# Where the x of the final addition comes from: four selecting matmuls from the norm's rows, in place of a second load

## The chip, the cores and the metric

The kernel runs on one core of a Trainium2 chip. A core has five engines with instruction queues of their own: TensorE (PE: matmuls, and PEld, its loads of weights), VectorE (DVE), ScalarE (ACT), GpSimd (POOL) and SyncE (SP). Sixteen DMA engines move data between the chip's memory and the core's SBUF. The metric is the device time of one execution in microseconds; lower is better.

## The reference

One decoding step for two sequences with a model width of 448: layer norm, attention over the last 2048 positions of a cache with 8 K/V heads of 256 and 16 query heads, and a gate from a two-layer network with relu. The attention's output is multiplied by the gate, and x is added.

```python
x = A_x                                   # (2, 1, 448)
xn = _layernorm(x, axis=-1)
# attention: q = xn @ wq, 16 heads of 256, W = 2048 of 8192 cached positions,
# softmax(q k^T / 16) v, then @ wo (4096 x 448)
s = _A_ref(xn, A_k_cache, A_v_cache, A_wq, A_wo)
# gate: silu(relu(xn @ w1) @ w2), w1 448 x 1792, w2 1792 x 448
g = _silu(_B_ref(xn, B_w1, B_w2))
return x + s * g
```

## The kernel before

The kernel writes one list of instructions for each engine (`_Prog`); an engine works its list in order and waits on semaphores for what an instruction depends on. Every instruction is recorded through the same helpers, so the profile names all DMA issues L36 and all matmuls L249.

**Loads.** SP issues, in this order: wq into `vbuf1` (L194), w1 and w2 into `vbuf0` (L195, L196), the K tiles 0 and 1 into `kbuf0` and `kbuf1`, then V 0, K 2, V 1, K 3, V 2, V 3 (`load_k`, `load_v`, L187 to L192), each as soon as the last reader of its buffer is done, and last wo in four parts into `kbuf0` (from L510). K and V come as four tiles of 4 MB each: a tile holds 32 stretches of 64 positions for each of four pairs of sequence and head on the 128 partitions.

**x.** ACT's queue begins with two loads of x. The first (L176) puts the two rows of 448 into partitions 0 and 1 of `x_sb`, for the norm. The second (L178, `d_xc`) puts x into `x_c` in the layout of the output: eight pieces of 112 numbers, piece i of row b in partition 32 i + 16 b. POOL clears `x_c` first (L177).

**Norm.** DVE takes mean and variance from `x_sb` (L212, L213), ACT the square root (L216), DVE the scaled rows `xg` (L219). PE turns them into columns in the PSUM bank `mbk` (L253), and DVE writes them to `xr` (L255). Between L219 and L255, DVE's list has the small constants made from the identity: `par8`, `wrow`, `wcol` (L230), `qmask` (L233), `fold`, `gsum`.

**Zeroing.** Before the square root ACT clears three PSUM banks (L210), `obk0`, `obk1` and `fbk`, since the matmuls with a column position write 4, 16 or 17 partitions of each group of 32.

**Body.** `do_q` multiplies wq (it waits for wq, `xr` and the cleared `obk0`). `do_H` (two halves), its transposes and `do_F` make the gate's input in `fbk`: four groups of 112 columns at partitions 0, 32, 64 and 96, 17 rows each, of which row 0 belongs to sequence 0 and row 16 to sequence 1. `do_gate` (ACT's exp at L328, then DVE) leaves the gate in `g_sb`. Then, for each K tile, DVE transposes it in eight steps (`do_T`, L343) and PE makes the scores (`do_S`); the softmax (`chain`) and the products with V (`do_PV`) of one tile run beside the scores of the next.

**End.** After the last V tile, 128 matmuls multiply wo into `fbk` (32 row groups, four column positions), DVE multiplies by the gate (L532) and adds `x_c` (L534), and ACT issues the store (L536).

`st` holds the last operation on each shared buffer, so that the next writer waits for it. It starts as `st = {"mbk": v_xr}` (L259): `fbk` has no earlier user than the zeroing, and `do_H` waits for that through `a_z[2]`.

Of the kernel before, what the change touches and what calls it, by code (L numbers as in the profile page):

```python
# [5 lines left out]
BF = mybir.dt.bfloat16  # L6
F32 = mybir.dt.float32
ACT = mybir.ActivationFunctionType
ALU = mybir.AluOpType
AX = mybir.AxisListType  # L10

PE, DVE, ACTE, SP, POOL = "pe", "dve", "act", "sp", "pool"
# [62 lines left out]
def bass_recurrent_scan__sliding_block_cached__dense_activation_relu__decode_kernel(  # L75
# [11 lines left out]
    B, Sq, D = A_x.shape  # L87
# [16 lines left out]
    NCOL = D // 4  # L104
# [4 lines left out]
    with es:  # L109
        pr = _Prog(nc, es)  # L110

        def named(name, shape, dt):
            return es.enter_context(nc.sbuf_tensor(name, shape, dt))

        def psum(name, shape, dt):
            return es.enter_context(nc.psum_tensor(name, shape, dt))

        def view(t, off, dims, n=128, p0=0, pstep=1):
            width = t.shape[1]
            return bass.AP(t, p0 * width + off, [[width * pstep, n]] + dims)  # L120

        ident = named("ident", [128, 128], BF)
# [10 lines left out]
        x_sb = named("x_sb", [128, D], BF)  # L133
# [7 lines left out]
        qbd = [named(f"qbd{i}", [128, QW], BF) for i in range(2)]  # L141
        h_n = named("h_n", [128, FC], BF)
        h_sb = named("h_sb", [128, 32], BF)
        x_c = named("x_c", [128, NCOL], BF)
        ea = named("ea", [128, NCOL], F32)
        g_sb = named("g_sb", [128, NCOL], F32)
        tmp = named("tmp", [128, NCOL], F32)
        out_sb = named("out_sb", [128, NCOL], BF)
# [20 lines left out]
        fbk = psum("fbk", [128, 512], F32)  # L169
        mbk = psum("mbk", [128, 512], F32)  # L170
        nbk = psum("nbk", [128, 512], F32)

        def kv_src(k, cache):
            return cache.rearrange("b h s d -> (b h) s d")[k::NQ, SK - W:SK, :].rearrange("g (i t) d -> i g (t d)", t=NT)

        d_x = pr.dma(ACTE, x_sb[0:B, :], A_x[:, 0, :])  # L176
        p_xc = pr.op(POOL, lambda e: e.memset(x_c[:, :], 0.0))  # L177
        d_xc = pr.dma(ACTE, view(x_c, 0, [[1, NCOL]], n=8, pstep=16),  # L178
                      A_x[:, 0, :].rearrange("b (i n) -> i b n", i=4), [p_xc])
        d_k, d_v = {}, {}  # L180

        wq_src = A_wq.rearrange("r (hf c) -> (r hf) c", hf=2).rearrange("(p s) c -> p (s c)", s=SLOTS)
# [7 lines left out]
        def load_v(k):  # L190
# [8 lines left out]
        p_id = pr.op(POOL, lambda e: e.affine_select(  # L199
            out=ident[:, :], in_=ident[:, :], compare_op=ALU.not_equal, fill=1.0,  # L200
            base=0, pattern=[[-1, 128]], channel_multiplier=1), [i0])
        i1 = pr.op(POOL, lambda e: e.memset(ident_f[:, :], 0.0), [p_id])
        p_idf = pr.op(POOL, lambda e: e.affine_select(
            out=ident_f[:, :], in_=ident_f[:, :], compare_op=ALU.not_equal, fill=1.0,
            base=0, pattern=[[-1, 128]], channel_multiplier=1), [i1])
        p_one = pr.op(POOL, lambda e: e.memset(one_f[:, :], 1.0), [p_idf])
        p_hz = pr.op(POOL, lambda e: e.memset(h_sb[:, :], 0.0))
        p_qz = [pr.op(POOL, lambda e, t=t: e.memset(t[:, :], 0.0)) for t in qbd][-1]

        a_z = [pr.op(ACTE, lambda e, t=t: e.memzero(t[:, :])) for t in (obk[0], obk[1], fbk)]  # L210
# [4 lines left out]
            out=sd[0:B, 0:1], in0=st2[0:B, 1:2], scalar1=EPS, scalar2=None, op0=ALU.add), [v_ag])  # L215
        a_sd = pr.op(ACTE, lambda e: e.activation(sd[0:B, 1:2], sd[0:B, 0:1], ACT.Sqrt), [v_ve])  # L216
        v_rs = pr.op(DVE, lambda e: e.reciprocal(rstd[0:B, :], sd[0:B, 1:2]), [a_sd])
        for e2 in range(2):
            v_xn = pr.op(DVE, lambda e, e2=e2: e.tensor_scalar(  # L219
                out=view(xg, 128 - 127 * e2, [[256, 4], [128, 2], [2, 64]], n=B),  # L220
                in0=view(x_sb, 3 * e2, [[1, 4], [0, 2], [SLOTS, 64]], n=B),
# [3 lines left out]
            out=par2[:, :], in_=view(ident, 0, [[1, 2], [2, 64]]), axis=AX.X, op=ALU.add), [p_id])  # L225
# [4 lines left out]
        v_wc = pr.op(DVE, lambda e: e.tensor_scalar(  # L230
            out=view(wcol, 0, [[4, 128], [1, 4]], n=4), in0=view(ident, 0, [[0, 128], [1, 4]], n=4),
            scalar1=1.0, scalar2=BIG, op0=ALU.subtract, op1=ALU.mult))
        v_qm = pr.op(DVE, lambda e: e.tensor_reduce(  # L233
            out=qmask[:, :], in_=view(ident, 0, [[32, 4], [1, 32]]), axis=AX.X, op=ALU.add))

# [12 lines left out]
        def mm(out_ap, lhsT, rhs, start, stop=False, **kw):  # L248
            return lambda e: e.matmul(out_ap, lhsT=lhsT, rhs=rhs, start=start, stop=stop,  # L249
                                      skip_group_check=True, **kw)  # L250

        for s in range(SLOTS):
            m_xr = pr.op(PE, mm(mbk[:, 2 * s:2 * s + 2], xg[0:B, 128 * s + 128:128 * s + 256], ident[0:B, 0:B], s == 0),  # L253
                         [v_xn, p_id])
        v_xr = pr.op(DVE, lambda e: e.tensor_tensor(  # L255
            out=view(xr, 0, [[4, SLOTS], [2, 2], [1, 2]]), in0=view(mbk, 0, [[2, SLOTS], [0, 2], [1, 2]]),
            in1=view(par8, 0, [[1, SLOTS], [1, 2], [0, 2]]), op=ALU.mult), [m_xr, v_par8])

        st = {"mbk": v_xr}  # L259

        def do_q():
            deps = [d_wq, v_xr, a_z[0]]
# [253 lines left out]
        deps = [st["at", NQ - 1], v_fold]  # L516
        for b in range(2):
            m_at = pr.op(PE, mm(mbk[:, 256 + 32 * b:288 + 32 * b], at_exp[:, 128 * b:128 * b + 128],
                                fold[:, :], b == 0, b == 1), deps + [st["mbk"]])
            deps = []  # L520
        v_at2 = pr.op(DVE, lambda e: e.tensor_copy(at2[:, :], mbk[:, 256:320]), [m_at])  # L521
        deps = [v_at2, st["g"]]
        landed = dict(d_wo)
        for j in range(32):
            deps = deps + [landed.get(j)]
            for i in range(4):
# [4 lines left out]
                deps = []  # L531
        v_t = pr.op(DVE, lambda e: e.tensor_tensor(  # L532
            out=tmp[:, :], in0=fbk[:, 0:NCOL], in1=g_sb[:, :], op=ALU.mult), [m_o, st["g"]])
        v_o = pr.op(DVE, lambda e: e.tensor_tensor(  # L534
            out=out_sb[:, :], in0=tmp[:, :], in1=x_c[:, :], op=ALU.add), [v_t, d_xc])
        d_o = pr.dma(ACTE, out[:, 0, :].rearrange("b (i n) -> i b n", i=4),  # L536
                     view(out_sb, 0, [[1, NCOL]], n=8, pstep=16), [v_o])
        pr.op(SP, None, [d_o])
# [30 lines left out]
```

## Time and profile before

| | us |
|---|---|
| median of 3 runs | 110.84 |
| the three runs | 110.48, 110.84, 110.93 |
| the profiled execution | 110.73 |
| its span, first to last instruction | 109.3 |

| engine | busy, us | share of the span |
|---|---|---|
| PE matmuls | 63.9 | 58% |
| PE loads of weights | 26.0 | 24% |
| DVE | 57.6 | 53% |
| ACT | 12.4 | 11% |
| POOL | 9.0 | 8% |

The page gives busy times of the engines, 40 equal slices of the span with the busy share of each in tenths, the DMA queues (q1 is SP's, q10 ACT's, q8 and q14 carry instructions), the chain of work that ended last, and groups of instructions. A timeline row has the start, the duration, the engine, the line, the operation with its output and input, and in brackets how long the engine was idle before it and what ended that. A row of windows has the busy time and count for PE, PEld, DVE, ACT and POOL, the granted clock of TensorE, the busy share of the DMA engines and their GB/s.

### The profile page before, as it was taken

To read this page: it belongs to the slowest core of one execution; us is meant where nothing else is said; L and a number is where in the kernel's file an instruction comes from. 1 tells how busy PE (TensorE), PEld (TensorE's weight loads), DVE (VectorE), ACT (ScalarE), POOL (GpSimd) and SP (SyncE) were. 2 spreads that over 40 slices of the span, in tenths; PEclk is the share of its full clock that TensorE was granted. 3 is DMA by queue.
4 is the path that set the end of the run, shared out by engine and by line. 5 is a ranking of instruction groups with operands and counts; after the bars stand their busy time and mean duration, and the time that the engine had idled before them with its cause. 6 is when DMAs were issued, how large, how long until landed. Compare 5 with 4: busy or idle time off the path is not lost.

```text
span 109.3 us, 1328 instructions
## 1 busy us (share of the span) xinstructions
PE 63.9 (58%) x554; PEld 26.0 (24%) x554; DVE 57.6 (53%) x95; ACT 12.4 (11%) x24; POOL 9.0 (8%) x45
## 2 busy tenths in 40 slices
PE   0010655764089897849481999683089949009491
PEld 0000113133033222323130334241034214003190
DVE  2165047320399999987435999242399943100202
ACT  2970000000000000200050000032000004100200
POOL 6500000720000004000500000000000000000000
PEclk9999999999556999999996559999959999955559
DMA  6898999999999999999999999999999999999940
GB/s 169 346 483 355 431 404 510 408 432 504 390 396 444 492 396 396 456 480 396 399 480 438 396 408 492 432 396 408 504 420 396 420 498 408 396 405 414 407 171 1
DMA packets 2321, 44.19 MB, mean 404 GB/s; under 512 B 266, under 2 KB 396, under 8 KB 908
## 3 DMA queue, kind: packets, MB, share of 16 engines
q1 hardware_dynamic: 2288, 44.11, 94.6%
q8 instruction: 4, 0.07, 0.2%
q10 hardware_dynamic: 28, 0.01, 0.0%
q14 instruction: 1, 0.01, 0.0%
HBM read 44.11 MB, written 0.00 MB: 403 GB/s over the span
## 4 chain that ended last, share of the span: by engine, by line
DMA 70%; DVE 12%; PE 12%; SPq 3%; issue 1%
DMA kbuf<-in_A_k_cache_dram 42%; DMA kbuf<-in_A_wo_dram 28%; DVE kt L343 10%; PE sbk L249 9%; SPq L36 3%; PE obk L249 2%; DVE tmp L331 1%; DVE rm L361 1%; PE mbk L249 0%; PE nbk L249 0%; PE fbk L249 0%; DVE mx L371 0%; DVE tmp L532 0%; PE mbk L366 0%; DVE out_sb L534 0%
## 5 line engine op out<-in xcount | busy, mean ns | idle before, releaser
L249 PE MATMUL sbk<-kt,qbd 128*128 128x512 bf16 x128 | 36.2, 432 | 15.0 <-DVE kt L343 14.5
L343 DVE STREAM_TRANSPOSE kt<-kbuf 128x1024 f32<-128x1024 f32 x32 | 36.9, 1210 | 8.9 <-DMA kbuf<-in_A_k_cache_dram 8.7
L249 PEld LDWEIGHTS sbk<-kt,qbd 128*128 128x128 bf16 x128 | 12.3, 107 | 37.2 <-DVE kt L343 22.5
L249 PE MATMUL obk<-vbuf,pt 128*16 128x512 bf16 x128 | 9.3, 442 | 4.6 <-DMA vbuf<-in_A_v_cache_dram 4.6
L292 POOL COPY qbd<-qall 32x32 bf16<-32x32 bf16 x32 | 5.7, 204 | 44.1 <-PE sbk L249 28.3
L383 ACT ACTIVATE bias<-mbk 128x1 f32<-128x1 f32 x4 | 0.7, 171 | 58.6 <-PE mbk L249 58.6
L433 DVE TENSOR_TENSOR at_exp<-nbk,qmask 128x16 bf16<-128x16 f32 x16 | 1.7, 166 | 10.5 <-PE nbk L249 10.5
L249 PE MATMUL obk<-vbuf,xr 128*4 128x512 bf16 x28 | 3.2, 626 | 3.8 <-DMA vbuf<-in_A_wq_dram 3.8
L392 DVE STREAM_TRANSPOSE pt<-e_sb 128x512 bf16<-128x512 bf16 x4 | 2.8, 711 | 4.7 <-ACT e_sb L387 4.7
L271 DVE TENSOR_SCALAR kt<-obk 128x1024 bf16<-128x1024 f32 x2 | 2.4, 1218 | 5.6 <-PE obk L249 5.6
L249 PEld LDWEIGHTS obk<-vbuf,pt 128*16 128x16 bf16 x128 | 3.1, 98 | 8.5 <-DMA vbuf<-in_A_v_cache_dram 4.7
L249 PE MATMUL mbk<-ident,xg 2*128 2x2 bf16 x7 | 0.3, 164 | 7.9 <-DVE xg L219 7.9
L361 DVE TENSOR_REDUCE rm<-sbk 128x1 f32<-128x512 f32 x4 | 2.7, 682 | 4.0 <-PE sbk L249 4.0
L249 PE MATMUL fbk<-vbuf,xr 128*4 128x448 bf16 x14 | 4.3, 461 | 0.7 <-DVE h_n L304 0.7
L416 ACT ACTIVATE o_sb<-obk,rs 128x512 bf16<-128x512 f32 x4 | 2.7, 687 | 11.1 <-PE obk L249 11.1
L249 PE MATMUL fbk<-kbuf,at 128*17 128x112 bf16 x128 | 3.1, 282 | 0.4 <-DVE at L521 0.3
L249 PEld LDWEIGHTS fbk<-kbuf,at 128*17 128x17 bf16 x128 | 2.7, 128 | 0.7 <-DVE at L521 0.4
L304 DVE TENSOR_SCALAR h_n<-fbk 4x448 bf16<-4x448 f32 x2 | 1.2, 612 | 3.0 <-PE fbk L249 3.0
L387 ACT ACTIVATE e_sb<-sbk,bias 128x512 bf16<-128x512 f32 x4 | 2.7, 687 | 0.1
L249 PE MATMUL mbk<-one_f,mrow 1*128 1x1 f32 x8 | 1.5, 256 | 1.9 <-DVE mrow L374 1.9
L366 PE MATMUL mbk<-ident_f,rm 128*1 128x128 f32 x4 | 1.1, 270 | 2.4 <-DVE rm L361 2.4
L249 PE MATMUL nbk<-fold,o_sb 128*128 128x8 bf16 x16 | 1.0, 170 | 2.2 <-ACT o_sb L416 2.2
(63 smaller groups left out, 34.4 us busy)
## 6 DMA issues: line engine op xcount, KB each, us to landing
kbuf<-in_A_k_cache_dram SPq DMA_DIRECT2D x4, 4096.0 KB, 27.0
vbuf<-in_A_v_cache_dram SPq DMA_DIRECT2D x4, 4096.0 KB, 26.4
vbuf<-in_A_wq_dram SPq DMA_DIRECT2D x1, 3584.0 KB, 11.2
vbuf<-in_B_w_dram SPq DMA_DIRECT2D x2, 1568.0 KB, 16.2
kbuf<-in_A_wo_dram SPq DMA_DIRECT2D x1, 1904.0 KB, 28.2
kbuf<-in_A_wo_dram SPq DMA_DIRECT2D x1, 1008.0 KB, 30.0
kbuf<-in_A_wo_dram SPq DMA_DIRECT2D x1, 448.0 KB, 30.6
kbuf<-in_A_wo_dram SPq DMA_DIRECT2D x1, 224.0 KB, 30.7
```

The lines of the kernel that those rows point to most:

```text
L36: o = _Op(eng, lambda e: e.dma_start(dst, src), [d for d in deps if d is not None], True)
L249: return lambda e: e.matmul(out_ap, lhsT=lhsT, rhs=rhs, start=start, stop=stop, skip_group_check=True, **kw)
L271: v = pr.op(DVE, lambda e, par=par: e.tensor_scalar(out=view(kt, 128 * par, [[256, 8], [32, 4], [1, 32]]), in0=view(obk[0], par, [[64, 8], ...
L292: st["qbd", k] = pr.op(POOL, lambda e, a=a, b=b: e.tensor_copy(view(qbd[k % 2], 24 + 32 * a + 4 * b, [[2, 2], [128, 8], [1, 2]], n=32, p0= ...
L304: st["h_n"] = pr.op(DVE, lambda e: e.tensor_scalar(out=h_n[0:4, u * (FC // 2):(u + 1) * (FC // 2)], in0=fbk[0:4, 0:FC // 2], scalar1=0.0, ...
L343: st["T", k, e] = pr.op(DVE, lambda e: e.transpose(view(dst, lo, [[128, NT // 2], [1, 32]]), view(src, lo, [[128, NT // 2], [1, 32]])), deps)
L361: st["rm", k] = pr.op(DVE, lambda e: e.tensor_reduce(out=rm[k % 2][:, :], in_=sbk[k % 2][:, :], axis=AX.X, op=ALU.max), [st["S", k, 7], st ...
L366: st["rmT", k] = pr.op(PE, lambda e: e.matmul(mbk[0:1, 0:128], lhsT=rm[k % 2][:, :], rhs=ident_f[:, :], start=True, stop=True, is_transpos ...
L387: st["exp", k] = pr.op(ACTE, lambda e: e.activation(e_sb[k % 2][:, :], sbk[k % 2][:, :], ACT.Exp, bias=bias[k % 2][:, 0:1], accum_out=ssum ...
L392: st["pt", k] = pr.op(DVE, lambda e: e.transpose(pt[k % 2][:, :], e_sb[k % 2][:, :]), [st["exp", k], st.get(("PV", k - 2))])
L416: st["osb", k] = pr.op(ACTE, lambda e: e.activation(o_sb[k % 2][:, :], obk[k % 2][:, :], ACT.Copy, scale=rs[:, k:k + 1]), [st["PV", k], st ...
L433: st["at", k] = st["nbk"] = pr.op(DVE, lambda e, b=b, h=h: e.tensor_tensor(out=view(at_exp, 128 * b + 64 * h + 16 * k, [[4, 2], [8, 2], [1 ...
```

## The change

The second load of x and the memset of its tile go. In their place a small matrix `sel` of ones and zeros is made: POOL clears its two rows, and DVE copies the 2 x 2 identity into its columns 0 and 16. Four matmuls, one for each 112 columns, multiply `sel` (2 x 17) with the raw rows of `x_sb` and write 17 rows at partitions 0, 32, 64 and 96 of `fbk`: row 0 is sequence 0, row 16 sequence 1, as in the gate. ACT copies the bank's 112 columns on all partitions to `x_c`, which is now a tile of f32. `fbk`'s next user waits for that copy, and the final addition for it instead of the load. The matmuls stand between the norm's transposes and `do_q` in PE's list; the copy to `sel` stands between `wcol` and `qmask` in DVE's; ACT's copy stands between the square root and the gate's exp.

```diff
@@ -141,7 +141,8 @@
         h_sb = named("h_sb", [128, 32], BF)
-        x_c = named("x_c", [128, NCOL], BF)
+        sel = named("sel", [128, 32], BF)
+        x_c = named("x_c", [128, NCOL], F32)
@@ -174,9 +175,6 @@
         d_x = pr.dma(ACTE, x_sb[0:B, :], A_x[:, 0, :])
-        p_xc = pr.op(POOL, lambda e: e.memset(x_c[:, :], 0.0))
-        d_xc = pr.dma(ACTE, view(x_c, 0, [[1, NCOL]], n=8, pstep=16),
-                      A_x[:, 0, :].rearrange("b (i n) -> i b n", i=4), [p_xc])
@@ -204,6 +202,7 @@
+        p_sz = pr.op(POOL, lambda e: e.memset(sel[0:B, :], 0.0))
         p_hz = pr.op(POOL, lambda e: e.memset(h_sb[:, :], 0.0))
@@ -230,6 +229,7 @@
+        v_sel = pr.op(DVE, lambda e: e.tensor_copy(view(sel, 0, [[16, 2]], n=B), ident[0:B, 0:B]), [p_sz, p_id])
@@ -256,7 +256,14 @@
-        st = {"mbk": v_xr}
+        deps = [d_x, v_sel, a_z[2]]
+        for i in range(4):
+            m_xc = pr.op(PE, mm(fbk[32 * i:32 * i + 17, 0:NCOL], sel[0:B, 0:17], x_sb[0:B, i * NCOL:(i + 1) * NCOL],
+                                True, True, tile_position=(0, 32 * i)), deps)
+            deps = []
+        a_xc = pr.op(ACTE, lambda e: e.activation(x_c[:, :], fbk[:, 0:NCOL], ACT.Copy), [m_xc])
+
+        st = {"mbk": v_xr, "fbk": a_xc}
@@ -532,7 +539,7 @@
         v_o = pr.op(DVE, lambda e: e.tensor_tensor(
-            out=out_sb[:, :], in0=tmp[:, :], in1=x_c[:, :], op=ALU.add), [v_t, d_xc])
+            out=out_sb[:, :], in0=tmp[:, :], in1=x_c[:, :], op=ALU.add), [v_t, a_xc])
```

## The prediction

> **What bounds the kernel now.** I read the page first: the span, the slices of DMA, the queues, and the chain that ended last.
>
> ```profile
> span 109.3 us, 1328 instructions
> PE 63.9 (58%) x554; PEld 26.0 (24%) x554; DVE 57.6 (53%) x95; ACT 12.4 (11%) x24; POOL 9.0 (8%) x45
> ...
> DMA  6898999999999999999999999999999999999940
> q1 hardware_dynamic: 2288, 44.11, 94.6%
> q8 instruction: 4, 0.07, 0.2%
> q10 hardware_dynamic: 28, 0.01, 0.0%
> HBM read 44.11 MB, written 0.00 MB: 403 GB/s over the span
> DMA 70%; DVE 12%; PE 12%; SPq 3%; issue 1%
> ```
>
> The 16 DMA engines are busy at nine tenths or more in nearly every slice from the second to the 38th of 40, and one queue, q1, takes 94.6% of them: that is SP's stream of weights, K and V, 44.11 MB. The queue that carries x and the output, q10, rounds to 0.0%. Of the chain, 70% is DMA. No compute engine bounds this kernel; the question for any edit is whether it moves the start, the rate or the end of that stream. The chain in order of time shows how far the stream runs ahead of the compute:
>
> ```profile
> 2.10 27.07 DMA kbuf<-in_A_k_cache_dram
> ...
> 39.68 19.32 DMA kbuf<-in_A_k_cache_dram
> ...
> 75.98 30.68 DMA kbuf<-in_A_wo_dram
> 106.65 0.04 issue
> 106.70 0.30 PE fbk L249 x8
> ...
> 107.03 0.28 DVE tmp L532
> ...
> 107.34 0.28 DVE out_sb L534
> ```
>
> A K tile is 4096 KB, which at 403 GB/s takes 10.4 us. The one issued at 39.68 landed after 19.32 us, so about 8.9 us of other transfers were queued ahead of it when it was issued. The compute that frees a buffer could run 8.9 us late before the engines had nothing to move. The end is the last part of wo landing at 106.65, eight matmuls, the gate multiply, the addition of x, and the store.
>
> **The start, where the edit is.** The timeline of the first 26 us:
>
> ```profile
> 0.73 0.19 POOL L177 MEMSET x_c<- 128x112 bf16 x1 [0.29 <-POOLq L554]
> 0.73 0.37 SPq L36 DMA_DIRECT2D vbuf<-in_A_wq_dram  x1
> 0.74 0.54 ACTq L36 DMA_DIRECT2D x_sb<-in_A_x_dram  x1
> ...
> 1.32 0.63 ACTq L36 DMA_DIRECT2D x_c<-in_A_x_dram  x1
> ...
> 1.99 1.28 ACT L210 ACT_TABLE_LOAD   x1 [1.99 <-POOL ident_f L202]
> ...
> 4.25 0.59 ACT L210 ACTIVATE fbk<-fbk 128x512 uint32<-128x512 uint32 x1
> ...
> 6.16 0.20 ACT L216 ACTIVATE sd<-sd 2x1 f32<-2x1 f32 x1
> ...
> 7.91 0.34 PE L249 MATMUL mbk<-ident,xg 2*128 2x2 bf16 x7 [7.91 <-DVE xg L219]
> ...
> 8.29 0.27 DVE L230 TENSOR_SCALAR wcol<-ident 4x512 bf16<-4x512 bf16 x1
> ...
> 9.49 0.18 DVE L255 TENSOR_TENSOR xr<-mbk,par 128x28 bf16<-128x28 f32 x1
> ...
> 12.02 3.16 PE L249 MATMUL obk<-vbuf,xr 128*4 128x512 bf16 x28 [3.77 <-DMA vbuf<-in_A_wq_dram]
> ...
> 18.16 2.77 PE L249 MATMUL fbk<-vbuf,xr 128*4 128x448 bf16 x7
> ...
> 25.74 0.26 ACT L328 ACTIVATE ea<-fbk 128x112 f32<-128x112 f32 x1 [18.09 <-PE fbk L249]
> ```
>
> xr, the last product of the norm, is ready at 9.67; the first matmuls that use it start at 12.02 because wq lands then. The norm has 2.35 us to spare. ACT's first work begins at 1.99, right behind the x_c issue (1.32 + 0.63 = 1.95).
>
> **Part by part.** *Removed: the load of x_c.* ACT's queue is 0.63 us shorter, so its zeroing, the square root, and with it xr can come up to 0.63 us earlier (if the label on L210, which names POOL, is right, only about 0.15 us, the removed memset and gap). In both cases the time is lost again to the wait for wq: 0. What the load took from the DMA engines is bounded by the next answer, the queues between 0 and 12 us, and by the rows of 0.5 us behind it.
>
> ```profile
> q10 hardware_dynamic: 16, 0.00, 0.1%
> ...
> 2.00:2.50 0.50, 0.00 (x0) 0.00 (x0) 0.44 (x1) 0.50 (x1) 0.43 (x4) 1.00 0.19 57
> 2.50:3.00 0.50, 0.00 (x0) 0.00 (x0) 0.43 (x3) 0.50 (x1) 0.50 (x2) 1.00 0.14 57
> 3.00:3.50 0.50, 0.00 (x0) 0.00 (x0) 0.06 (x1) 0.49 (x2) 0.50 (x2) 1.00 0.60 229
> ```
>
> Both x loads together took 0.1% of 16 engines in 12 us, 0.19 us of engine time. If x_c had it all, on the one engine that ends last, the stream would end 0.19 us sooner; spread over several engines, a few hundredths. I take 0.02 us. (A last column of 57 to 229 GB/s shows a slow start of the stream from 2.0 to 3.5, just after the x_c issue; that is the first rival.) No SP issue is moved past anything: x is ACT's queue.
>
> *Added before the stream's first use.* POOL gets a small memset in place of a larger one, DVE a 2-partition copy, PE four matmuls, ACT one copy out of fbk. The nearest rows:
>
> ```profile
> L249 PE MATMUL fbk<-kbuf,at 128*17 128x112 bf16 x128 | 3.1, 282 | 0.4 <-DVE at L521 0.3
> L207 POOL MEMSET h_sb<- 128x32 bf16 x1 | 0.1, 124 | 0.0
> L228 DVE COPY wrow<-ident 4x128 bf16<-4x128 bf16 x1 | 0.2, 206 | 0.0
> L332 DVE TENSOR_TENSOR g_sb<-fbk,tmp 128x112 f32<-128x112 f32 x1 | 0.3, 273 | 0.0
> L534 DVE TENSOR_TENSOR out_sb<-tmp,x_c 128x112 bf16<-128x112 f32 x1 | 0.3, 275 | 0.0
> ```
>
> The memset: 0.12 in place of 0.19. The copy into sel: at most 0.21, in DVE's queue ahead of xr, so xr comes at 9.67 + 0.21 = 9.88 at worst and near 9.2 with ACT's 0.63 gained; wq's landing at 12.02 covers both. The four selecting matmuls have the shape of the wo ones in columns: between 4 x 0.024 = 0.1 us (3.1 us over 128) and 4 x 0.28 = 1.1 us; I take 0.4, nearer to a short burst. They stand behind the transposes of 7.91 and ahead of the q matmuls, and they wait for sel (about 8.6 + 0.2) and for fbk's zeroing (ends at 4.84). Behind them on PE only the q matmuls are queued, which wait until 12.02. Even 1.1 us from 9.0 ends at 10.1. The copy to x_c is 0.26 by the row of ea (same shape, same bank), ending near 10.4 at worst; ACT has nothing else until 25.74, and fbk's next writer comes at 18.16. Were ACT to switch its table once more for the copy, 1.28 us would lie in the same 15 us. Without the cover of wq (2.35 us), sel and the matmuls would cost 0.3 to 1.3 us.
>
> *The end.* The addition now reads two f32 operands from SBUF instead of one f32 and one bf16. The multiply of f32 by f32 (L332) took 273 ns against 275: 0. Its wait for the load becomes a wait for a copy done some 95 us earlier: 0.
>
> *The sum.* The profiled execution took 110.73 us, its span 109.3 and 1.43 around it. 110.73 - 0.02 = 110.71. The runs shown have a median of 110.84, which is 0.11 above that execution, so the forecast is 110.84 - 0.02 = 110.8. The three runs lie between 110.48 and 110.93, so the likeliest case's own range is 110.4 to 111.1.
>
> **Rivals.** *Faster: the x_c issue held up the stream's start.* For it: the 1.5 us of low rate from 2.0 follow the issue, and both queues feed the same engines. Against: wq was issued at 0.73, ahead of x_c, and the 0.1% of q10 is too little to fill the gap. If the whole 0.63 us of ACT's issue is a delay of SP's stream, and the 0.19 comes with it, the end moves by up to 0.82: 110.0 to 110.2. The tail limits more than that:
>
> ```profile
> 103.86 3.12 PE L249 MATMUL fbk<-kbuf,at 128*17 128x112 bf16 x128 [0.32 <-DVE at L521]
> 106.70 0.11 PEld L249 LDWEIGHTS fbk<-kbuf,at 128*17 128x17 bf16 x8 [0.23 <-DMA kbuf<-in_A_wo_dram]
> ```
>
> The wo matmuls waited only 0.23 us for their last part, so a stream that ended sooner in its last part alone would win 0.23 us at most.
>
> *Slower: the stream's buffers move.* sel (32 x 2 bytes) and the wider x_c (112 x 2 bytes more) are declared ahead of every K and V buffer, so these move by 288 bytes in each partition, which is no multiple of 64. If rows that start elsewhere cost the transfers something, all 44.11 MB pay. A price from rows: 16 small packets took 0.19 us, 12 ns each (6 to 18 with the rounding of 0.1%). If each of the 2288 packets of q1 paid that once more, each of 16 engines would lose 2288 x 12 / 16 = 1.7 us (0.9 to 2.6): 112.5. It decides, beyond 0.5%, from 0.55 x 16 / 2288 = 3.8 ns a packet. Against it:
>
> ```profile
> 100.00:104.00 4.00, 2.37 (x34) 0.75 (x26) 0.64 (x5) 0.69 (x1) 0.00 (x0) 0.50 0.97 407
> ```
>
> wo's second part starts 17 x 448 x 2 = 15232 bytes into its buffer, a multiple of 128 and not of 256; in the window where it moves, the engines stay at 407 GB/s, the mean of the span. A shift of 32 bytes against 64 is not in that row.
>
> [...]
>
> *No less traffic than before: the added instructions bring a fetch.* q8's four instruction packets took 0.2% of 16 x 109.3 us, 3.5 us, 0.87 each. PE has eight more instructions (four loads of weights, four matmuls). If these call for a fifth packet, and on the engine that ends last: +0.87, 111.7. Against: eight are few beside the 1108 that PE already has (554 matmuls, 554 loads of weights).
>
> **How the numbers follow.** No change 0.60; the start held up 0.18; moved buffers 0.15; a fetch 0.07. Half a per cent, about what a measurement of this kernel tells from no change, is 0.55 us: 110.29 to 111.39. The first case lies inside, the second below it, the last two above. So faster 0.18, same 0.60, slower 0.22. The range of 110.1 to 111.8 takes in the first case, most of the second and the fetch, and leaves out the moved buffers at 112.5 and the lowest end: under 0.2.
>
> **What would show it.** Right: q1's share and the GB/s over the span unchanged, the first q matmul still at about 12.0 behind wq, the four matmuls and ACT's copy done by 10.4, the last part of wo landing at 106.4 to 106.9, the addition at 275 ns. Wrong on the fast side: the first q matmul earlier by half a microsecond, with more GB/s from 2.0 to 3.5. Wrong on the slow side: a lower rate in every window of 4 us (moved buffers), or five packets in q8 and a late last part of wo.

## The result and the profile after

The changed kernel took 111.21 us (median of 6 runs, 111.13 to 111.38), the kernel before 110.73 (6 runs, 110.37 to 110.93). The ratio is 1.0054, with a 95% interval of 1.0041 to 1.0068: slower by 0.48 us between the medians and by 0.60 us as the ratio has it, just past the half per cent that the prediction took as the bound.

The page of the changed kernel, span and queues (packets, MB, share of 16 engines):

```profile
span 110.0 us, 1337 instructions
...
q1 hardware_dynamic: 2288, 44.11, 94.5%
q8 instruction: 4, 0.07, 0.2%
q14 instruction: 1, 0.01, 0.0%
q10 hardware_dynamic: 16, 0.00, 0.0%
HBM read 44.11 MB, written 0.00 MB: 401 GB/s over the span
```

The second load is gone: q10 has 16 packets where it had 28. SP's stream has the same packets and bytes, but its packets now keep the engines busy for 94.5% of 110.0 = 103.95 us, where it was 94.6% of 109.3 = 103.4 us. The engines are no idler than before; the same bytes need more time.

The start of the changed kernel, its timeline:

```profile
1.31 1.28 ACT L209 ACT_TABLE_LOAD   x1 [1.31 <-PEq L561]
...
2.27 0.12 POOL L205 MEMSET sel<- 2x32 bf16 x1
...
7.81 0.15 DVE L232 COPY sel<-ident 2x2 bf16<-2x2 bf16 x1
...
8.06 0.27 PE L249 MATMUL fbk<-x_sb,sel 2*17 2x112 bf16 x4 [0.49 <-issue]
...
8.38 0.26 ACT L264 ACTIVATE x_c<-fbk 128x112 f32<-128x112 f32 x1 [2.70 <-PE fbk L249]
8.66 1.28 ACT L335 ACT_TABLE_LOAD   x1
...
8.88 0.18 DVE L255 TENSOR_TENSOR xr<-mbk,par 128x28 bf16<-128x28 f32 x1
...
12.29 3.16 PE L249 MATMUL obk<-vbuf,xr 128*4 128x512 bf16 x28 [3.96 <-DMA vbuf<-in_A_wq_dram]
```

Everything that was added is done by 8.64, xr by 9.06, and the q matmuls still wait for wq, now for 3.96 us. The added work costs nothing here. wq itself lands 0.27 us later than in the first profile of before; the experiments show how much of that is spread.

The chain of the changed kernel in order of time, and the last loads of weights:

```profile
2.09 27.48 DMA kbuf<-in_A_k_cache_dram
...
40.07 19.34 DMA kbuf<-in_A_k_cache_dram
...
74.69 23.81 DMA vbuf<-in_A_v_cache_dram
...
104.26 3.37 PE fbk L249 x128
...
107.97 0.27 DVE out_sb L541
```

```profile
107.23 0.12 PEld L249 LDWEIGHTS fbk<-kbuf,at 128*17 128x17 bf16 x8 [0.24 <-DMA kbuf<-in_A_wo_dram]
```

The addition takes 0.27 us as before. Of the 0.63 us by which it starts later (107.97 against 107.34), 0.53 are there at the last part of wo, whose loads of weights start at 107.23 against 106.70. K 0 lands 0.40 us later in this pair of profiles (29.57 against 29.17), but experiment 4 shows that this point can't carry a reading. Compute waits for nothing new: the transposes are idle for 8.9 us ahead of K in both, the products with V for 4.3 us ahead of V against 4.6; what is late is the data.

### The profile page after: what moved, and what is told of

Its sections match the earlier page's. It is cut to its first block, busy times and chain, and to the rows that moved or that the text cites. A ratio compares the mean times of both kernels' runs of the same rounds, so it can differ in the third digit from the quotient of the medians.

```text
span 110.0 us, 1337 instructions
## 1 busy us (share of the span) xinstructions
PE 65.4 (59%) x558; PEld 26.6 (24%) x558; DVE 57.6 (52%) x96; ACT 12.7 (12%) x25; POOL 9.0 (8%) x45
## 3 DMA queue, kind: packets, MB, share of 16 engines
q1 hardware_dynamic: 2288, 44.11, 94.5%
## 4 chain that ended last, share of the span: by engine, by line
DMA 64%; PE 18%; DVE 13%; SPq 1%; issue 1%; ACT 1%
DMA kbuf<-in_A_k_cache_dram 43%; DMA vbuf<-in_A_v_cache_dram 22%; DVE kt L350 9%; PE sbk L249 9%; PE obk L249 5%; PE fbk L249 3%; SPq L36 1%; DVE tmp L338 1%; DVE rm L368 1%; ACT o_sb L423 1%; PE mbk L249 1%; DVE at_exp L440 0%; PE nbk L249 0%; DVE mx L378 0%; DVE tmp L539 0%
## 5 line engine op out<-in xcount | busy, mean ns | idle before, releaser
L249 PE MATMUL sbk<-kt,qbd 128*128 128x512 bf16 x128 | 37.3, 444 | 14.6 <-DVE kt L350 14.2
L350 DVE STREAM_TRANSPOSE kt<-kbuf 128x1024 f32<-128x1024 f32 x32 | 36.9, 1210 | 8.9 <-DMA kbuf<-in_A_k_cache_dram 8.9
```

The costliest lines, as they stand in the source:

```text
L350: st["T", k, e] = pr.op(DVE, lambda e: e.transpose(view(dst, lo, [[128, NT // 2], [1, 32]]), view(src, lo, [[128, NT // 2], [1, 32]])), deps)
```

## The experiments

All ratios are to the kernel before, run beside it on the same chip. They come with a 95% interval in brackets and differ a little from the quotients of the medians. The list of tiles that the builder makes gives the places of the stream's buffers in a partition, in bytes:

```
          kbuf0    past a multiple of 256
before    39168      0
after     39456     32      (sel 64 bytes, x_c wider by 224: 288 more)
```

The theories: the moved buffers (the prediction's slow rival), the start (the missing load or ACT's earlier work changes how the stream begins), and the added work.

**1. The kernel before, with its buffers where the changed kernel has them.**

```diff
+        pad = named("pad", [128, 144], BF)
         x_c = named("x_c", [128, NCOL], BF)
```

> The kernel before, with one unused tile of 288 bytes a partition declared ahead of x_c, so that every later buffer, K and V among them, starts where it starts in the changed kernel. Nothing else differs. Addresses theory: the loss belongs to the moved buffers, so this kernel takes about 0.5 us more than before (ratio 1.004 to 1.007), with wq's first matmul at about 12.3 in place of 12.02. Start theory (the loss comes from taking the second load of x out of the start, or from ACT starting sooner): ratio 1.000, first q matmul at 12.0. Added work theory (matmuls, copies, instructions): ratio 1.000.

Measured: 111.24 against 110.53 us, ratio 1.0058 (1.0044 to 1.0072). One unused tile makes the whole loss, with the second load of x still in place and no matmul added. The point at 12.3 was a miss: the q matmuls begin at 12.06.

**2. The changed kernel, with its buffers where the kernel before has them.**

```diff
-        sel = named("sel", [128, 32], BF)
-        x_c = named("x_c", [128, NCOL], F32)
+        hole = named("hole", [128, NCOL], BF)
...
         kt = named("kt", [128, ROW], BF)
+        sel = named("sel", [128, 32], BF)
+        x_c = named("x_c", [128, NCOL], F32)
```

> The changed kernel, with sel and the f32 x_c declared behind all other tiles and an unused tile of the old x_c's 224 bytes in its place, so that every other buffer starts where it starts before the change. Addresses theory: the loss is gone, ratio to before 1.000 (0.999 to 1.001). Start theory and added work theory: the loss stays, ratio 1.004 to 1.007.

Measured: 110.55 against 110.53 us, ratio 0.9999 (0.9990 to 1.0008). The loss is gone, and what remains of the change, four matmuls in place of a load, is worth nothing within 0.1%.

**3. The changed kernel, with the second load of x put back beside it.** The load goes to a spare tile that nothing reads.

```diff
+        x_old = named("x_old", [128, NCOL], BF)
...
+        p_xc = pr.op(POOL, lambda e: e.memset(x_old[:, :], 0.0))
+        d_xc = pr.dma(ACTE, view(x_old, 0, [[1, NCOL]], n=8, pstep=16),
+                      A_x[:, 0, :].rearrange("b (i n) -> i b n", i=4), [p_xc])
...
```

> The changed kernel with the second load of x put back (memset and eight pieces, at their old places in POOL's and ACT's lists) into a spare tile declared last, which nothing reads; the x that is added still comes from the matmuls. Start theory: the loss is gone, ratio to before 1.000, first q matmul at 12.0. Addresses theory and added work theory: ratio 1.004 to 1.007, first q matmul at 12.3.

Measured: 111.18 us, ratio 1.0053 (1.0039 to 1.0068), the same as the changed kernel without it. The start theory falls. The point at 12.3 was missed again: 12.11.

**4. The kernel before, once more**, for the spread of what a profile shows.

> The kernel before, once more, for the spread of its profile: first q matmul at 12.02, K 0 landing at 29.2, V 3 at 98.1, wo's last part at 106.65 in the first profile. All theories: ratio 1.000; if these points move by 0.3 us from one execution to the next, the places at which the changed kernel lost time can't be read from one profile of each.

Measured: 110.54 us, ratio 1.0000 (0.9989 to 1.0010). The start of the q matmuls in two profiles, first this kernel, then the changed kernel with its buffers at home:

```profile
11.93 1.45 PE L249 MATMUL obk<-vbuf,xr 128*4 128x512 bf16 x12 [3.69 <-DMA vbuf<-in_A_wq_dram]
```

```profile
11.78 1.45 PE L250 MATMUL obk<-vbuf,xr 128*4 128x512 bf16 x12 [3.45 <-DMA vbuf<-in_A_wq_dram]
```

With buffers at home they begin anywhere from 11.78 to 12.02, in kernels of the same time, and with moved buffers from 11.82 (run 5) to 12.29. So the 0.27 us at wq in the changed kernel's profile is no sign of a loss by itself; a point early in one profile of each kernel does not carry a reading of 0.3 us. K 0 was expected at 29.2 and moved most. In this second profile of the same kernel it lands at 30.26, 1.09 us later than in the first, in a run that took 110.60 us against 110.73:

```profile
2.09 28.17 DMA kbuf<-in_A_k_cache_dram
```

The end of the stream is steadier. By the trace's packet records the last packet of wo ends at 106.01 to 106.21 us in the five profiles whose buffers start on a multiple of 256 (both of before, runs 2, 6 and 10), and at 106.53 to 106.74 in the four that start 32 past one (the changed kernel, runs 1, 3 and 5). Between the means of the two groups lie 0.51 us.

**5 and 6. Which tiles: the stream's buffers alone, or the small tiles alone.** In run 5 only kbuf and vbuf are moved, by 32 bytes.

```diff
+        pad = named("pad", [128, 16], BF)
         kbuf = [named(f"kbuf{i}", [128, ROW], BF) for i in range(2)]
         vbuf = [named(f"vbuf{i}", [128, ROW], BF) for i in range(2)]
+        pad2 = named("pad2", [128, 112], BF)
         kt = named("kt", [128, ROW], BF)
```

> The kernel before with only the four buffers that the stream fills (kbuf, vbuf) moved, by 32 bytes a partition; the small tiles ahead of them and kt stay at their places against 256 bytes. Theory of the stream's rows (a row that starts off a boundary costs its transfer something): ratio to before 1.004 to 1.007, as with the move of 288, which is 32 past a multiple of 256. Theory of the engines' tiles (DVE, PE or ACT read or write moved tiles more slowly): ratio 1.000.

In run 6 the tiles from x_c on are moved by 288 bytes, and kbuf, vbuf and kt by 512.

```diff
+        pad = named("pad", [128, 144], BF)
         x_c = named("x_c", [128, NCOL], BF)
...
+        pad2 = named("pad2", [128, 112], BF)
         kbuf = [named(f"kbuf{i}", [128, ROW], BF) for i in range(2)]
```

> The counterpart: the small tiles from x_c on are moved by 288 bytes, as in the changed kernel, and kbuf, vbuf and kt by 512, so that they start on a multiple of 256 again. Theory of the stream's rows: ratio 1.000. Theory of the engines' tiles: 1.004 to 1.007, if it is the small tiles.

Measured: the stream's buffers alone, 111.20 us, ratio 1.0054 (1.0036 to 1.0071); the small tiles alone, 110.57 us, ratio 0.9997 (0.9985 to 1.0008). The loss belongs to the buffers that DMA fills. It is not that DVE reads K more slowly and frees kbuf later: a transpose out of kbuf takes 1210 ns in the kernel before and in run 5.

```profile
L343 DVE STREAM_TRANSPOSE kt<-kbuf 128x1024 f32<-128x1024 f32 x32 | 36.9, 1210 | 8.9 <-DMA kbuf<-in_A_k_cache_dram 8.7
```

```profile
L345 DVE STREAM_TRANSPOSE kt<-kbuf 128x1024 f32<-128x1024 f32 x32 | 36.9, 1210 | 8.6 <-DMA kbuf<-in_A_k_cache_dram 8.6
```

The rate of the whole stream on the two pages, run 5 first:

```profile
HBM read 44.11 MB, written 0.00 MB: 402 GB/s over the span
```

```profile
HBM read 44.11 MB, written 0.00 MB: 404 GB/s over the span
```

**7 to 10. How far they are moved.** Run 5's diff with other widths (64, 128 and 224 bytes), and a move of 256 with kt moved along.

> As the run with 32 bytes, but the four buffers moved by 64. If the boundary that counts is 256 bytes: ratio 1.004 to 1.007. If it is 64 bytes: ratio 1.000. Theory of the engines' tiles: 1.000.

> As before, moved by 128. Boundary of 256 bytes: ratio 1.004 to 1.007. Boundary of 128 or 64 bytes: ratio 1.000. Theory of the engines' tiles: 1.000.

> The kernel before with the four stream buffers moved by 224 bytes, that is 32 short of the next multiple of 256, and kt at home. If the cost of a row depends only on its starting off the boundary: about as with 32 or 128 bytes, ratio 1.003 to 1.006. If it grows with the bytes between the boundary below and the start (the bytes that a first piece skips): more than with 32, ratio 1.006 or above. If it falls with the bytes that are left to the next boundary, as 0.65, 0.57 and 0.40 us at 32, 64 and 128 suggest: about 0.1 us, ratio 1.000 to 1.002.

> The kernel before with kbuf, vbuf and kt moved by 256 bytes, the size of the boundary that the other moves suggest. Boundary of 256 bytes: ratio 1.000. A larger boundary (512 bytes): the four buffers go from 256 past a multiple of 512 to a multiple of it, so the kernel would be faster than before, ratio 0.994 to 0.998.

| moved by | median, us | over before, us | ratio (95% interval) |
|---|---|---|---|
| 32 | 111.20 | 0.67 | 1.0054 (1.0036 to 1.0071) |
| 64 | 111.10 | 0.57 | 1.0039 (1.0024 to 1.0054) |
| 128 | 110.93 | 0.40 | 1.0033 (1.0022 to 1.0043) |
| 224 | 111.20 | 0.60 | 1.0053 (1.0038 to 1.0067) |
| 256 | 110.62 | 0.06 | 1.0001 (0.9992 to 1.0011) |

Among these moves the boundary is 256 bytes: the four off it cost 0.40 to 0.67 us, the move by the whole of it costs nothing, and its buffers, at 39424, start on a multiple of 512 and are no faster (1.0001). At 64 and 128 the ratio came out below the 1.004 to 1.007 that was expected. The idea that the cost falls with the bytes left to the next boundary (from 32, 64 and 128) was wrong: 224 costs what 32 costs, 0.60 and 0.67 us. So the cost does not grow with the bytes between the boundary and the start either. That 64 and 128 cost less than 32 can't be told from these times, whose intervals overlap; the packet records below show it. A move by 128 brings 16 of an engine's 128 rows onto the boundary, the second halves of w2 and the second part of wo, which start 128 past it at home. The records show that this is not why it costs less: these rows are no shorter there.

**11 and 12. Is the cost paid once a row?** Each K and V load is issued as four loads of a quarter of every row, with the buffers at home and moved by 32.

```diff
-            d_k[k] = pr.dma(SP, kbuf[k % 2][:, :], kv_src(k, A_k_cache), [st.get(("T", k - 2, 7))])
+            d_k[k] = [pr.dma(SP, kbuf[k % 2][:, lo:lo + ROW // 4], kv_src(k, A_k_cache)[:, :, lo:lo + ROW // 4],
+                             [st.get(("T", k - 2, 7))]) for lo in range(0, ROW, ROW // 4)]
...
```

The V loads are cut in the same way.

> The kernel before with each of the eight K and V loads issued as four loads of a quarter of each row, so that a tile comes as 512 rows of 8192 bytes in place of 128 of 32768. Buffers at home. It is the base for the next run. Where a row has a fixed cost, this kernel is slower than before for the extra rows alone; both theories allow any ratio from 1.00 to 1.03.

> The same four loads for each tile, with the four stream buffers moved by 32 bytes. To be read against the run with the same loads at home. If the off-boundary cost is paid once for each row: the engines have 335 rows each where they had 143, so the loss of 0.6 us grows to about 1.4 us. If it is paid once for each 256-byte piece, or by bytes: the loss stays at 0.6 us.

Measured: at home 111.55 us, moved by 32 bytes 113.18 us (ratios to before 1.0089, 1.0072 to 1.0106, and 1.0236, 1.0216 to 1.0256). The move now costs 1.63 us where it cost 0.67; about 1.4 was expected if each row pays. Windows of 4 us in mid-stream, at home first (the last two columns are the share of the DMA engines and GB/s):

```profile
40.00:44.00 4.00, 3.38 (x15) 1.00 (x14) 3.99 (x5) 0.00 (x0) 1.43 (x8) 1.00 1.01 428
60.00:64.00 4.00, 2.61 (x7) 0.93 (x8) 3.92 (x4) 0.00 (x0) 0.00 (x0) 0.53 1.01 422
80.00:84.00 4.00, 3.38 (x8) 1.15 (x9) 4.00 (x5) 0.00 (x0) 0.00 (x0) 0.50 1.01 428
```

```profile
40.00:44.00 4.00, 3.66 (x16) 1.16 (x14) 3.98 (x5) 0.00 (x0) 1.42 (x8) 1.00 1.01 420
60.00:64.00 4.00, 1.80 (x5) 0.68 (x6) 3.10 (x3) 0.00 (x0) 0.00 (x0) 0.74 1.01 418
80.00:84.00 4.00, 2.16 (x6) 0.77 (x7) 3.46 (x4) 0.00 (x0) 0.00 (x0) 0.50 1.02 422
```

The engines are busy all the time in both, and move 0.9% to 1.9% less when the rows start off the boundary. The rows themselves can be counted: of q1's 2288 packet records, in the kernel before and in the changed one, 2048 are rows of 1792 to 32768 bytes, 16 for each of 128 partitions, and 240 have 4 bytes, 16 for each of the 15 loads, which are taken here as one completion on each engine; so an engine has 128 rows on the mean, and 320 with the quarters. (The expectation counted completions too, 143 and 335, and left out 24 of the quarters' loads.) Spread over all rows, the cost is 0.67 / 128 = 5.2 ns a row and 1.63 / 320 = 5.1 ns a row; by the intervals of the ratios they are good to about 1.5 ns and 1 ns. The bytes did not change and the loss grew with the rows, so the cost is not paid once a byte or once for each 256 bytes.

The packet records of the trace show the same from inside. Mean duration of a packet by size, ns:

```
bytes in a row     32768    8192   15232    8064    3584    1792   12544    6272
(loads)            K, V    K, V/4   wo 1    wo 2    wo 3    wo 4      w1      w2
home (run 4; 11)  1215.0   309.5   568.0   305.1   140.0    74.0   469.9   239.0
moved 32 (5; 12)  1219.8   314.9   569.2   311.8   144.3    75.6   469.0   239.0
moved 64 (run 7)  1218.6           568.8   311.5   143.2    75.0   469.0   239.0
moved 128 (run 8) 1217.3           569.8   306.1   141.3    74.5   469.0   239.0
moved 224 (run 9) 1219.9           575.9   306.0   143.2    75.7   469.0   239.0
moved 256 (10)    1215.0           568.0   305.1   140.0    74.0   469.0   239.0
```

A K or V row is 4.8 ns longer, a quarter row 5.4. The rows of w1 and w2, at the start of the stream, are no longer at all, although they go to the same moved buffers. So 5 ns is a mean over rows that pay and rows that don't. Over an engine's rows, K and V make 64 x 4.8 = 0.31 us and wo 0.11 us, 0.42 of the 0.51 by which the stream ends later.

Which rows of wo pay depends on both of their ends. The first part is 59.5 times 256 bytes long. At home, and moved by 32, 64 or 128, it touches 60 stretches between multiples of 256, and the moves cost it 0.8 to 1.8 ns; moved by 224 it touches 61 and pays 7.9 ns. The second part starts 128 past a multiple at home and touches 32. Moved by 32 or 64 it touches 33 and pays 6.7 and 6.4 ns; moved by 128 or 224 it touches 32 and pays 1.0 and 0.9. A whole K or V row touches 128 on the boundary and 129 off it, wherever it starts. So among these rows most of the cost goes with one more stretch touched, and 224 is like 32 for K and V. This is read from the records; no run tested it by itself.

At 128 a K or V row is only 2.3 ns longer. By eighths of these rows in the order of their start, about a tile each, the first three are as at home (means of 1213.0, 1216.8 and 1213.5 ns against 1213.0, 1216.6 and 1213.0 in run 4), and the other five are 3.2 to 4.2 ns longer. Why the rows of w1 and w2, and at 128 the first tiles, are spared stays open, and so does the rest of the 0.67.

## Why the prediction was wrong

**What bounds the kernel.** Right, and it decided: DMA is the bound (q1 took 94.6% of the 16 engines' span before and 94.5% after), so the only thing in this edit that could matter was what touches the stream.

**The parts that were costed at nothing.** Right, nearly each number. The memset took 0.12, the copy to sel 0.15 (at most 0.21 forecast), the four matmuls 0.27 (0.4), ACT's copy 0.26, the table switch fell behind it (1.28 us from 8.66) and was hidden, the addition stayed at 0.27. ACT began 0.68 us sooner, which the wait for wq swallowed. Put together, run 2: 0.9999.

**The removed load.** Right within the measurement: 0.02 us forecast, nothing found (run 2 against before, run 3 against the changed kernel). Behind the first rival's slow start from 2.0 to 3.5 us there is no delay by the load: without the load, at home addresses, nothing is gained. The slow start is there without it too: in run 2 the same three half microseconds run at 57, 57 and 287 GB/s (the last column).

```profile
2.00:2.50 0.50, 0.00 (x0) 0.00 (x0) 0.03 (x1) 0.50 (x1) 0.44 (x5) 1.00 0.17 57
2.50:3.00 0.50, 0.00 (x0) 0.00 (x0) 0.50 (x1) 0.49 (x2) 0.50 (x1) 1.00 0.16 57
3.00:3.50 0.50, 0.00 (x0) 0.00 (x0) 0.40 (x3) 0.50 (x2) 0.50 (x2) 1.00 0.70 287
```

**The sum.** This is the step that failed: "110.73 - 0.02 = 110.71". It went through the diff's operations and put its declarations at nothing, though the slow rival named them. sel and the wider x_c move every buffer behind them by 288 bytes, and this term, +0.6 us, belongs into the sum. The forecast of no change at 110.8 was 0.4 us short, though 111.21 lies inside the range of 110.1 to 111.8.

**The slow rival.** The mechanism was named with its place and got 0.15. Two things kept it there. Its price was 1.7 us, since it took the 12 ns of a tiny packet for each of 2288 packets; what was measured is 5.2 ns on the mean of 2048 rows. With 5.2 x 2048 / 16 = 0.67 us in place of 1.7 the case would have stood at 111.5. And the row that was read against it could not speak against it: wo's second part starts 128 bytes off the boundary, and the window with it ran at 407 GB/s, near the mean of 403. But this part ends on a multiple of 256, and its packets are no shorter when it starts on one too (306.1 ns in run 8 against 305.1). And the whole loss is half a per cent, which no window of 4 us shows. The prediction's sign, a lower rate in every such window, could not be seen: from 40, 60 and 80 us the kernel before has 442, 401 and 459 GB/s, and the changed kernel 418, 442 and 410.

**The other rivals.** No fetch was added: q8 has four packets before and after in every profile of the two kernels. The tail is bound by data and compute at once, as forecast: the wo matmuls waited 0.24 us for their last part, against 0.23 before. But that part came at about 107.2, past the 106.4 to 106.9 of the forecast, late with the whole stream.

## What to carry to other kernels

When a kernel is bound by DMA, read a diff's declarations like its instructions: a new tile ahead of the big buffers moves them, and 288 unused bytes alone cost 0.6 us here. Print where the buffers that DMA fills start, pad so that they start on a multiple of 256 bytes (the starts that lost nothing here), and test an edit with the buffers held in place before its operations are blamed or praised; here the edit itself is worth nothing either way. Declaring them first would not have done it: the builder puts this kernel's first tile at 16512, which is 128 past a multiple of 256. Long rows did better twice here: rows off the boundary paid about 5 ns each on the mean, and cutting K and V rows from 32768 to 8192 bytes cost 0.99 us even at home.

## What the runs showed of the hardware

A stream whose rows start 32 or 224 bytes past a multiple of 256 in SBUF took 0.67 and 0.60 us longer over 128 rows an engine, and 1.63 us over 320, about 5 ns for each row on the mean. At 64 and 128 it was less (0.57 and 0.40 us), at 256 nothing (0.06, ratio 0.9992 to 1.0011). The rows do not pay alike: one of 32768 bytes is 4.8 ns longer at 32 and 2.3 at 128. The rows of wo's first two parts are 6.4 to 7.9 ns longer where a row touches one more stretch of 256 bytes, and 0.8 to 1.8 where it does not. The rows of w1 and w2, early in the stream, are no longer (469.0 and 239.0 ns against 469.9 and 239.0). The four-part loads at home add 192 rows and 24 completions to each engine for 0.99 us, 5 ns for each row if the rows carry it all. And the start of an identical stream varies between profiles: in kernels with buffers at home and equal times, wq's matmuls began between 11.78 and 12.02 us, and K 0 landed at 29.17 and at 30.26 in two profiles of one kernel.
